# A small product for the sums of the exponentials, its inverse and its broadcast, one slot later

## The chip, the cores and the metric

The kernel runs on one core of a Trainium2 chip. The engines named below are TensorE (PE; its weight loads are a row of their own, PEld), VectorE (DVE), ScalarE (ACT), GpSimd (POOL) and the queue from which most transfers are issued (SP). The metric is the time of one execution on the device in microseconds (us): the median of three runs of the kernel before is 901.06 us.

## The reference

Soft-capped attention, and then a mixing block on its output:

```python
scores = scale * np.matmul(q, k.transpose(0, 1, 3, 2))      # q, k, v: batch 8, heads 12, 448 x 64
scores = cap * np.tanh(scores / cap)
attn = np.exp(scores - max);  attn = attn / (np.sum(attn, axis=-1, keepdims=True) + 1e-09)
x = np.matmul(attn, v)                                      # heads side by side: batch 8, 448 x 768
theta = x @ w_theta
yr = w_tok_r @ (x * cos(theta));  yi = w_tok_i @ (x * sin(theta))
u = x + yr + yi
out = u + np.maximum(u @ w_ch, 0.0)
```

## The kernel before, in words

Two heads make a pair, so there are 48 pairs, six for each of the eight batches. The program is a hand-written pipeline of slots. Slot s computes the scores, the tanh and the exponentials of pair s, and the product with V, the row sums and the normalisation of earlier pairs. Beside that, each slot from the ninth on carries one sixth of the mixing block of one batch that is already through attention. Six slots in a row ("parts" 0 to 5) so hold the mixing block of batch b and the attention of six later pairs.

The order inside a slot is a string of words in `part_scripts`, and the words are emitted in that order; each engine then runs its own instructions strictly in the order in which they were emitted. The words that matter here, with the lines of the profile:

- `SA`, `SB`: the score matmuls of the first and second half of the keys (L262, L279) and their tanh on ACT (L297); `SB` emits the matmuls and `tB` the tanh. `A`, `B`: the exponentials on ACT (L308, L303, L305).
- `V`: the product of the exponentials with V for the pair before (L368); `x` copies it out (L387); `v` loads a further V from ACT's queue (L232).
- `a`, `b` and `a-`, `b-`: the exponentials are added up over the blocks of keys on DVE (L332, L334) and reduced to `part` (L322). The words with a minus do it for the pair of the slot before. `c`, `c-`: for every second pair, the rest of the keys is reduced (L322, `rest`) and added into `part` (L356).
- `r`: a small product on PE (L400, 56 x 32 out) that finishes the row sums of two pairs from `part`. `inv`: their reciprocal on DVE (L436) and a transfer of 7 KB to a buffer in HBM (L441). `bc`: four transfers that read that buffer back, broadcast to 128 partitions (L457). `norm`: two multiplications on DVE that use them (L461).
- `prep`: DVE splits the next queries and keys into a high and a low part (L221, L222). `q`, `q+`: loads of queries and keys on SP (L209).
- `mix0` to `mix5`: the six mixing products of the batch, 21 matmuls each (L545 to L547), from `zh` (`high`, ACT, L531) and `zl` (`low`, DVE, L537); `gain0` to `gain5` add them to x on DVE (L551), `us` splits the sum for the last product (L471, L472), `ch` is that last product.

PE's outputs `r`, `mx`, `th`, `ch` and the product with V of odd pairs share one pool of three PSUM buffers, in the order of emission; a product waits until the buffer of the third one before it has been read.

Of the kernel before, what the change touches and what calls it, by code (L numbers as in the profile page):

```python
# [36 lines left out]
def softcap_attn_then_spectral_mix(ctx, tc, qk2, v, vj, cap, w_theta, w_tok, w_ch, sel, outT):  # L37
    nc = tc.nc
    B, NP, P, _, S = qk2.shape
# [155 lines left out]
    vt, pt, bc = {}, {}, {}  # L195
# [186 lines left out]
    def copy_x(k):  # L382
        if joint(k) and k % 2 == 0:
            return
        for n in (k - 1, k) if joint(k) else (k,):
            x = wk.tile([P, S], F32, tag="x", name=f"x{n}", bufs=12)
            nc.scalar.copy(x, ACC.pop(n)[:, :S])  # L387
            X[n // NP, n % NP] = x
# [3 lines left out]
    def direct(k):  # L392
        return k < DIRECT and not state["general"]

    def sums(k, halves=(0, 1)):

        if not direct(k):
            if k % 2 == 1 and 0 in halves:
                state["r"] = psM.tile([P, 512], F32, tag="m", name=f"r{k}")
                nc.tensor.matmul(state["r"][: 4 * TB, :32], parts.pop(k).rearrange("p n t -> p (n t)"), sel_sb, start=True, stop=True)  # L400
            return
        alone = NP <= k
        if not alone and k % 2 == 0:
            return
        if (k % 2 == 0 or not alone) and 0 in halves:
            state["r"] = psM.tile([P, 512], F32, tag="m", name=f"r{k}")
        r = state["r"]
        for c in range(NCH):
            if c // 2 in halves:
                for n in (k,) if alone else (k - 1, k):  # L410
                    for hh in range(2):
                        i = 2 * (n % 2) + hh
                        nc.tensor.matmul(r[32 * i : 32 * i + 32, :S], ones_sb, pt[n, c // 2][:CP, c % 2, hh, :],
                                         start=c == 0, stop=c == NCH - 1)
# [5 lines left out]
    def invert(k):  # L420

        if k % 2 == 0:
            return
        r = state.pop("r")
        ri = wk.tile([4 * TB, 32], F32, tag="rq", name=f"rq{k}", bufs=1)
        if direct(k):
            rows = wk.tile([P, S + D], F32, tag="ri", name=f"ri{k}", bufs=1)[:, :S]
            nc.vector.tensor_copy(rows, r[:, :S])
            nc.sync.dma_start(ri, rows[::32, :].rearrange("n (t i) -> n t i", i=32))
            summed[k] = ri  # L430
            return
        if state["general"]:
            nc.vector.tensor_scalar_add(ri, r[: 4 * TB, :32], 1e-9)
            nc.vector.reciprocal(ri, ri)
        else:
            nc.vector.reciprocal(ri, r[: 4 * TB, :32])  # L436
        keep(k, ri)

    def keep(k, ri):
        inverse[k] = dram.tile([2, 2, S], F32, tag="inverse", name=f"inverse{k}")  # L440
        nc.sync.dma_start(inverse[k].rearrange("n h (t i) -> (n h t) i", i=32), ri)  # L441

    def inverted(k):
        if k in summed:
            ri = summed.pop(k)
            nc.vector.reciprocal(ri, ri)
            keep(k, ri)

    def spread(k):
        inverted(k)  # L450
        if k not in inverse:
            return
        rows = inverse.pop(k)
        for n in (k - 1, k):
            bc[n] = wk.tile([P, S], F32, tag="bc", name=f"bc{n}", bufs=2)
            for hh in range(2):
                nc.sync.dma_start(bc[n][hh * D : (hh + 1) * D, :], rows[n % 2, hh : hh + 1, :].broadcast_to([D, S]))  # L457

    def norm(k):
        x = X[k // NP, k % NP]  # L460
        nc.vector.tensor_tensor(x, bc.pop(k), x, op=ALU.mult)  # L461
# [104 lines left out]
    def part_scripts(b):  # L566
        rows = [
# [9 lines left out]
        ]  # L577
        if b == 0:
            rows = [
# [9 lines left out]
            ]  # L589
        return [row.split() for row in rows]  # L590
# [75 lines left out]
    def slot(s):  # L666
        k = s - 1
        b, part = divmod(s - FIRST, 6) if s <= NS else (B - 1, None)
        live = s < NS
        tail = k < NS  # L670
        tanh = {}

        def do(e):
            if e == "SA" and live:
                qk_half(s, 0)()
            if e == "SAm" and live:
                tanh["A"] = qk_half(s, 0)
            if e == "tA" and live:
                tanh["A"]()
            if e == "V" and tail:  # L680
                av(k)
            if e == "x" and tail:
                copy_x(k)
            if e == "v" and s + 1 < NS:
                load_v(s + 1)
            if e == "r" and tail:
                sums(k)
            if e == "inv" and tail:
                invert(k)
            if e == "bc" and tail:  # L690
                spread(k)
            if e == "SB" and live:
                tanh[0] = qk_half(s, 1)
            if e == "tB" and live:
                tanh[0]()
            if e == "prep" and WHOLE <= s + 1 < NS:
                split_qk(s + 1)
            if e == "q":
                if s >= WHOLE:
                    if live and s % 2 == 0:  # L700
                        load_ends(s)
                    if s % 2 == 1 and s + 1 < NS:
                        load_qk(s + 1)
                elif s + 2 < NS:
                    load_qk(s + 2)
            if e == "q+" and s >= WHOLE and s + 2 < NS:
                load_qk(s + 2)
            if e in ("wa", "wb", "wc", "wd", "we"):
                weights(s, e[1])
            if e in ("A", "B") and live:  # L710
                exp_half(s, "AB".index(e))
            if e in ("a", "b") and live:
                add_half(s, "ab".index(e))
            if e in ("a-", "b-") and tail:
                add_half(k, "ab".index(e[0]))
            if e == "c" and live:
                add_ends(s)
            if e == "c-" and tail:
                add_ends(k)
            if e == "norm":  # L720
                if s % 2 == 1 and s < NS:
                    norm(s - 3)
                    norm(s - 2)
                if s == NS:
                    norm(s - 2)
                    norm(s - 1)
                    for j in range(NJ):
                        split_x(B - 1, j, "xs")

        for e in TAIL[s - NS - 1].split() if s > NS else part_scripts(b)[part]:  # L730
            name = e.rstrip("0123456789")
            if name in WORK:
                WORK[name](b, int(e[len(name):]))
            else:
                do(e)
# [76 lines left out]
```

## Time and profile before

| | |
|---|---|
| median of 3 runs | 901.06 us (899.86 to 902.13) |
| the profiled execution | 905.79 us, of which the trace spans 904.0 us |
| TensorE's mean granted clock in it | 0.989 of full speed |
| busy: PE, PEld, DVE, ACT | 878.6, 644.6, 658.3, 562.9 us |

Busy times are unions of the instructions of an engine. A matmul's end is modelled, so that matmuls that follow each other closely overlap in the trace: their pace is read from their starts. An idle time stands in square brackets behind an instruction in a timeline, with what ended it.

### The profile page before, as it was taken

How to read it: one execution, taken by the hardware profiler on the slowest of the kernel's cores; microseconds unless marked ns; L12 is line 12 of the kernel's file. 1: busy time of each engine (PE TensorE's matmuls, PEld its weight loads, DVE VectorE, ACT ScalarE, POOL GpSimd, SP SyncE). 2: the span in 40 equal slices, each digit the busy share in tenths (PEclk: the TensorE clock that was granted, in tenths of full speed). 3: DMA queues.
4: the chain of work that ended last, by engine and by line, in shares of the span. 5: the costliest groups of instructions: out<-in, count | busy, mean ns of one | idle time of the engine just before them, and what ended most of it. 6: DMA issues, size and time to landing. Idle time of an engine off the chain costs nothing.

```text
span 904.0 us, 12434 instructions
## 1 busy us (share of the span) xinstructions
PE 878.6 (97%) x4780; PEld 644.6 (71%) x4780; DVE 658.3 (73%) x940; ACT 562.9 (62%) x582; POOL 1.1 (0%) x7
## 2 busy tenths in 40 slices
PE   8999999999999999999989999999989999999997
PEld 5333766776677776777767777767766776689997
DVE  5888899888775777755986569756787478864851
ACT  6987876668664695556953677446765559554320
POOL 0000000000000000000000000000000000000000
PEclk9999999999999999999999999999999999999999
DMA  7564284325523255222552325423362335501521
GB/s 265 189 202 123 85 279 152 127 95 163 161 77 111 77 183 183 66 100 84 181 168 85 104 100 178 131 84 116 112 191 86 105 95 166 159 15 51 194 82 64
DMA packets 70307, 117.32 MB, mean 130 GB/s; under 512 B 10464, under 2 KB 49888, under 8 KB 70240
## 3 DMA queue, kind: packets, MB, share of 16 engines
q1 hardware_dynamic: 64624, 107.47, 37.2%
q10 hardware_dynamic: 5616, 8.98, 3.4%
q8 instruction: 39, 0.64, 0.3%
q14 instruction: 28, 0.23, 0.1%
HBM read 83.18 MB, written 33.20 MB: 129 GB/s over the span
## 4 chain that ended last, share of the span: by engine, by line
PE 68%; DVE 15%; ACT 6%; DMA 4%; issue 3%; SPq 3%; DVEq 0%; ACTq 0%; POOL 0%; POOLq 0%
PE a L368 8%; PE s L262 7%; PE ch L480 6%; PE ch L482 6%; PE ch L481 6%; PE mx L545 5%; PE mx L546 4%; PE mx L547 4%; PE th L480 4%; PE th L481 4%; PE th L482 4%; DVE g_sb L508 4%; DMA g_sb<-turn 3%; DVE g_sb L515 3%; ACT p L297 3%
## 5 line engine op out<-in xcount | busy, mean ns | idle before, releaser
L297 ACT ACTIVATE p<-s,qscale 128x1792 f32<-128x1792 f32 (+1 forms) x96 | 153.6, 1600 | 145.4 <-PE s L262 117.2
L545 PE MATMUL mx<-wtk_h,zh 128*128 128x448 f32 x336 | 124.4, 370 | 0.0
L547 PE MATMUL mx<-wtk_h,zl 128*128 128x448 f32 x336 | 122.8, 366 | 0.0
L546 PE MATMUL mx<-wtk_l,zh 128*128 128x448 f32 x336 | 122.8, 365 | 0.0
L480 PE MATMUL th<-xs,wth_h 128*128 128x448 f32 x288 | 106.7, 370 | 0.0
L480 PE MATMUL ch<-us,wch_h 128*128 128x448 f32 x288 | 106.6, 370 | 0.0
L482 PE MATMUL ch<-us,wch_l 128*128 128x448 f32 x288 | 105.3, 366 | 0.2 <-DVE wch_l L138 0.2
L481 PE MATMUL ch<-us,wch_h 128*128 128x448 f32 x288 | 105.2, 365 | 0.0
L482 PE MATMUL th<-xs,wth_l 128*128 128x448 f32 x288 | 105.2, 365 | 0.0
L481 PE MATMUL th<-xs,wth_h 128*128 128x448 f32 x288 | 105.2, 365 | 0.0
L368 PE MATMUL a<-p,v 128*64 128x448 f32 x480 | 104.5, 573 | 0.0
L308 ACT ACTIVATE p<-p,cap_sb 128x1792 f32<-128x1792 f32 (+1 forms) x56 | 100.0, 1785 | 0.5
L559 DVE SCALAR_TENSOR_TENSOR x<-ch,x 128x448 f32<-128x448 f32 x48 | 29.7, 619 | 75.1 <-PE ch L482 75.1
L537 DVE TENSOR_TENSOR zl<-g_sb,zh 128x896 fp32r<-128x896 f32 x48 | 51.6, 1084 | 33.9 <-ACT zh L531 30.5
L368 PEld LDWEIGHTS a<-p,v 128*64 128x64 f32 x480 | 32.5, 144 | 56.0 <-issue 44.6
L545 PEld LDWEIGHTS mx<-wtk_h,zh 128*128 128x128 f32 x336 | 63.1, 188 | 12.4 <-issue 3.6
L508 DVE TENSOR_TENSOR g_sb<-g_sb,x 128x896 f32<-128x896 f32 x48 | 51.7, 1077 | 27.2 <-ACT g_sb L504 27.2
L547 PEld LDWEIGHTS mx<-wtk_h,zl 128*128 128x128 f32 x336 | 63.1, 188 | 5.2
L546 PEld LDWEIGHTS mx<-wtk_l,zh 128*128 128x128 f32 x336 | 63.1, 188 | 4.9
L480 PEld LDWEIGHTS th<-xs,wth_h 128*128 128x128 f32 x288 | 54.1, 188 | 11.7 <-issue 4.9
L480 PEld LDWEIGHTS ch<-us,wch_h 128*128 128x128 f32 x288 | 54.1, 188 | 10.6 <-issue 5.1
L531 ACT CAST zh<-g_sb 128x896 fp32r<-128x896 f32 x48 | 44.8, 939 | 25.8 <-PE mx L546 13.2
(103 smaller groups left out, 1450.3 us busy)
## 6 DMA issues: line engine op xcount, KB each, us to landing
turn<-g_sb SPq DMA_DIRECT2D x48, 448.0 KB
g_sb<-turn SPq DMA_DIRECT2D x192, 112.0 KB
qk_sb<-in_qk SPq DMA_DIRECT2D x39, 448.0 KB
bc<-inverse SPq DMA_DIRECT2D x96, 112.0 KB
out_dram<-x SPq DMA_DIRECT2D x48, 224.0 KB
v<-in_vj ACTq DMA_DIRECT2D x20, 256.0 KB
g_sb<-in_wth SPq DMA_DIRECT2D x6, 768.0 KB
ends<-in_qk SPq DMA_DIRECT2D x17, 256.0 KB
```

The lines of the kernel that those rows point to most:

```text
L262: nc.tensor.matmul(sp[:, i, hh, :S], kk[k][rows, 1, at : at + P], qq[k][rows, 0, :], start=n == 0, stop=n == 2)
L297: return lambda: nc.scalar.activation(pp[rows, :n], sp[rows, :n, :, :S], AF.Tanh, scale=qscale[rows])
L308: nc.scalar.activation(pp[rows], pp[rows], AF.Exp, scale=cap_sb[rows])
L368: nc.tensor.matmul(acc[hh * D : (hh + 1) * D, :S], va[:, c, hh, :], pt[k, c // 2][:, c % 2, hh, :], start=c == 0, stop=False)
L480: nc.tensor.matmul(acc[:, :S], wh[:, j, ms], t[:, 0, :], start=j == 0, stop=False)
L481: nc.tensor.matmul(acc[:, :S], wh[:, j, ms], t[:, 1, :], start=False, stop=False)
L482: nc.tensor.matmul(acc[:, :S], wl[:, j, ms], t[:, 0, :], start=False, stop=j == NJ - 1)
L508: nc.vector.tensor_tensor(g, g, X[b, j].unsqueeze(1).broadcast_to([P, 2, S]), op=ALU.mult)
L537: nc.vector.tensor_tensor(zl.rearrange("p c (g t) -> p c g t", g=4), turned(j), zh.bitcast(F32).rearrange("p c (g t) -> p c g t", g=4), op ...
L545: nc.tensor.matmul(acc[:, :S], zh[:, c, :], wtk_h[:, c, :], start=c == 0, stop=False)
L546: nc.tensor.matmul(acc[:, :S], zh[:, c, :], wtk_l[:, c, :], start=False, stop=False)
L547: nc.tensor.matmul(acc[:, :S], zl[:, c, :], wtk_h[:, c, :], start=False, stop=c == NC2 - 1)
```

## The change

It touches the scripts of parts 2 and 3 for batches 1 to 6 (batch 0 and the tail have scripts of their own). The words `r inv bc` leave the end of part 2 and stand in part 3 as `r- a inv- bc-`: the product behind `mix3`, the fourth mixing product; the reciprocal behind `a`; the broadcast behind that. `prep` moves from ahead of `gain3` to behind `us0`. Nothing is computed that was not computed before, and no instruction is added or taken away.

```diff
             "SA high0 low0 high1 sincos1 low1 b- V x v SB mix0 high2 rotate3 turn3 low2 gain0 tB q rotate4 turn4 back3 prep"
-            " rotate5 turn5 back4 back5 A B mix1 gain1 c- mix2 r inv bc",
-            "SA a- gain2 high3 low3 V x v high4 low4 SB tB q b- A mix3 a high5 low5 prep gain3 us0 q+"
+            " rotate5 turn5 back4 back5 A B mix1 gain1 c- mix2",
+            "SA a- gain2 high3 low3 V x v high4 low4 SB tB q b- A mix3 r- a inv- bc- high5 low5 gain3 us0 prep q+"
             " B mix4 b c gain4 us1 us2 norm mix5",
...
+            if e == "r-":
+                sums(k - 1)
+            if e == "inv-":
+                invert(k - 1)
+            if e == "bc-":
+                spread(k - 1)
```

On PE, at the first of the six places, the kernel before has the small product (`r`) between the last matmuls of `mix2` (`mx_2`) and the scores of the next slot (`s`):

```order
L545 MATMUL mx_2_1907<-wtk_h,zh_2_1842 128x448
L546 MATMUL mx_2_1907<-wtk_l,zh_2_1842 128x448
L547 MATMUL mx_2_1907<-wtk_h,zl_2_1848 128x448
L400 MATMUL r_1929<-sel_sb,part_1598 56x32
L262 MATMUL s<-hi_1862 128x448 x2
```

In the changed kernel the scores follow `mix2` at once, and at the end of `mix3` (`mx_3`), ahead of `mix4` (`mx_4`), the same engine has:

```order
L545 MATMUL mx_3_1979<-wtk_h,zh_3_1945 128x448
L546 MATMUL mx_3_1979<-wtk_l,zh_3_1945 128x448
L547 MATMUL mx_3_1979<-wtk_h,zl_3_1947 128x448
L400 MATMUL r_2001<-sel_sb,part_1598 56x32
L545 MATMUL mx_4_2029<-wtk_h,zh_4_1958 128x448
```

The product has moved behind the scores, the product with V and `mix3`.

On DVE the kernel before has, from the reciprocal (`rq`) on to `gain3` (the second `x`; the first is `gain2`):

```order
L436 RECIPROCAL rq_1931<-r_1929 56x32
L332 TENSOR_TENSOR psz<-p_0_1782 128x896
L551 TENSOR_TENSOR x_936<-mx_2_1907,x_936 128x448
L537 TENSOR_TENSOR zl_3_1959<-g_sb_94,zh_3_1957 128x896
L537 TENSOR_TENSOR zl_4_1972<-g_sb_94,zh_4_1970 128x896
L334 TENSOR_TENSOR psz<-psz,p_1_1819 128x896
L322 TENSOR_REDUCE part_1987<-psz 128x28
L332 TENSOR_TENSOR psz<-p_0_1953 128x896
L537 TENSOR_TENSOR zl_5_2016<-g_sb_94,zh_5_2014 128x896
L221 CAST hi_2018<-qk_sb 128x896
L222 TENSOR_TENSOR lo_2019<-qk_sb,hi_2018 128x896
L551 TENSOR_TENSOR x_938<-mx_3_1991,x_938 128x448
```

The changed kernel has there:

```order
L332 TENSOR_TENSOR psz<-p_0_1782 128x896
L551 TENSOR_TENSOR x_936<-mx_2_1907,x_936 128x448
L537 TENSOR_TENSOR zl_3_1947<-g_sb_94,zh_3_1945 128x896
L537 TENSOR_TENSOR zl_4_1960<-g_sb_94,zh_4_1958 128x896
L334 TENSOR_TENSOR psz<-psz,p_1_1819 128x896
L322 TENSOR_REDUCE part_1975<-psz 128x28
L332 TENSOR_TENSOR psz<-p_0_1941 128x896
L436 RECIPROCAL rq_2004<-r_2001 56x32
L537 TENSOR_TENSOR zl_5_2016<-g_sb_94,zh_5_2014 128x896
L551 TENSOR_TENSOR x_938<-mx_3_1979,x_938 128x448
L472 TENSOR_TENSOR us_0_2019<-x_567,us_0_2019 128x448
L221 CAST hi_2022<-qk_sb 128x896
```

The reciprocal has moved down by seven instructions, and `hi` and `lo` (the word `prep`) now stand behind `gain3` and the first `us`.

On SP's queue, as a difference from the kernel before, behind the last transfers of the rotated values (`turn`):

```order
 L523 DMA g_sb_94<-turn_5_1868 32x4x224 x4
-L441 DMA inverse_1933<-rq_1931 56x32
-L457 DMA bc_1935<-inverse_1933 64x448 x2
-L457 DMA bc_1938<-inverse_1933 64x448 x2
-L209 DMA qk_sb<-in_qk 128x896 x2
+L209 DMA qk_sb<-in_qk 128x896
+L441 DMA inverse_2006<-rq_2004 56x32
+L457 DMA bc_2008<-inverse_2006 64x448 x2
+L457 DMA bc_2011<-inverse_2006 64x448 x2
+L209 DMA qk_sb<-in_qk 128x896
```

The inverse and its four broadcasts have moved from ahead of the slot's two loads of queries and keys to between them.

## Rows read from the trace of the kernel before

**Rows 1.** The page: busy time, share of the span and instructions of each engine.
```profile
PE 878.6 (97%) x4780; PEld 644.6 (71%) x4780; DVE 658.3 (73%) x940; ACT 562.9 (62%) x582; POOL 1.1 (0%) x7
```

**Rows 2.** Waits of PE: us in total, times, longest.
```profile
PE r L400 <- DVE part L356: 14.7, 6, 3.0
```

**Rows 3.** Timeline of PE, first and fifth place: start, us, instruction [idle before].
```profile
239.05 0.37 PE L547 MATMUL mx<-wtk_h,zl 128*128 128x448 f32 x1
241.45 0.29 PE L400 MATMUL r<-sel_sb,part 128*56 128x32 f32 x2 [2.04 <-DVE part L356]
241.67 0.47 PE L262 MATMUL s<-hi 64*128 64x448 f32 x2
...
672.09 0.37 PE L547 MATMUL mx<-wtk_h,zl 128*128 128x448 f32 x1
675.41 0.29 PE L400 MATMUL r<-sel_sb,part 128*56 128x32 f32 x2 [2.96 <-DVE part L356]
```

**Rows 4.** Windows from the scores to `mix3`: us, busy, PEclk, DMA share, GB/s.
```profile
241.67:248.80 7.13, 7.13 (x41) 3.08 (x39) 3.17 (x5) 3.52 (x3) 0.00 (x0) 0.76 0.57 154
350.20:357.41 7.21, 7.21 (x41) 3.00 (x39) 3.16 (x5) 3.52 (x3) 0.00 (x0) 0.76 0.52 152
458.92:464.46 5.54, 5.54 (x40) 2.52 (x38) 3.07 (x4) 3.02 (x3) 0.00 (x0) 1.00 0.63 170
566.35:573.47 7.12, 7.12 (x41) 3.31 (x39) 3.15 (x5) 3.52 (x3) 0.00 (x0) 0.76 0.57 141
675.63:682.74 7.11, 7.11 (x41) 3.33 (x39) 3.18 (x5) 3.52 (x3) 0.00 (x0) 0.76 0.54 150
783.74:790.91 7.17, 7.17 (x40) 2.98 (x38) 4.98 (x6) 3.42 (x3) 0.00 (x0) 0.76 0.52 150
```

**Rows 5.** Timeline of PE where scores follow a mixing product directly.
```profile
261.71 0.37 PE L547 MATMUL mx<-wtk_h,zl 128*128 128x448 f32 x1
262.01 0.47 PE L262 MATMUL s<-hi 64*128 64x448 f32 x2
```

**Rows 6.** Timeline of DVE, third place.
```profile
458.25 0.40 DVE L356 TENSOR_TENSOR part<-part,rest 64x28 f32<-64x28 f32 x2
459.03 0.35 DVE L436 RECIPROCAL rq<-r 56x32 f32<-56x32 f32 x1 [0.38 <-PE r L400]
...
463.06 1.09 DVE L537 TENSOR_TENSOR zl<-g_sb,zh 128x896 fp32r<-128x896 f32 x1 [2.03 <-ACT zh L531]
...
468.35 1.09 DVE L332 TENSOR_TENSOR psz<-p 128x896 f32<-128x896 f32 x1
...
470.81 0.62 DVE L221 CAST hi<-qk_sb 128x896 fp32r<-128x896 f32 x1
...
472.47 0.62 DVE L551 TENSOR_TENSOR x<-mx,x 128x448 f32<-128x448 f32 x1
...
478.83 1.16 DVE L461 TENSOR_TENSOR x<-bc,x 128x448 f32<-128x448 f32 x2
...
483.73 1.70 DVE L472 TENSOR_TENSOR us<-x,us 128x448 fp32r<-128x448 f32 x3 [3.21 <-ACT us L471]
```

**Rows 7.** Timeline of PE, third place: end of `mix4`, start of `mix5`.
```profile
472.88 0.36 PE L547 MATMUL mx<-wtk_h,zl 128*128 128x448 f32 x1
473.08 0.36 PE L545 MATMUL mx<-wtk_h,zh 128*128 128x448 f32 x1
```

**Rows 8.** Timeline of SP's queue, first place.
```profile
244.17 0.36 SPq L441 DMA_DIRECT2D inverse<-rq  x1
246.36 3.35 SPq L457 DMA_DIRECT2D bc<-inverse  x4
249.81 7.54 SPq L209 DMA_DIRECT2D qk_sb<-in_qk  x2
```

**Rows 9.** Timeline of DVE: reciprocal and `norm` of the next two pairs.
```profile
269.95 0.35 DVE L436 RECIPROCAL rq<-r 56x32 f32<-56x32 f32 x1
...
279.56 1.15 DVE L461 TENSOR_TENSOR x<-bc,x 128x448 f32<-128x448 f32 x2
```

## The prediction

> **What bounds the kernel now.** I read four views, from coarse to fine. The busy times come first: PE is busy for 97% of the span, DVE for 73% and ACT for 62% [rows 1]. The reader is to see that a change pays only if PE waits less, or runs faster while it is busy. So the second view is the list of PE's waits. One entry stands out: the small product `r` waits six times for `part`, the last of DVE's row sums, 14.7 us in all and 3.0 us at most [rows 2]. The third is PE's timeline around one such wait. The last matmul of `mix2` starts at 239.05, then PE is idle for 2.04 us until DVE has written `part`, `r` runs at 241.45, and the next scores start at 241.67 [rows 3]. Nothing in those scores needs `r`; they stand behind it only because PE runs in order. The fourth view is the windows from those scores to `mix3`. The same matmuls take 5.54 us at the third place, where the granted clock is 1.00, and 7.11 to 7.21 us at the other five, where it is 0.76, a mean of full speed and of half of it [rows 4]. Of TensorE's two levels, 1.2 and 2.4 GHz, the lower one was granted for a part of these stretches, right behind the idle time. So each wait costs twice: once as idle time, and at five of six places again as slow matmuls.
>
> **The change part by part.** A place is one of the six batches, 1 to 6, in which the moved words stand.
>
> *The wait of `r` goes.* Without it the scores start 0.30 us after the last matmul of a mixing product, as they do where they follow one directly [rows 5]. Before, they start 241.67 - 239.05 = 2.62 us after it, that is 2.32 us later: the idle 2.04 and 0.28 for the modelled end of the last matmul and for `r` itself. For six places that is 14.7 + 6 x 0.28 = 16.4 us.
>
> *`r` is paid elsewhere.* It runs between `mix3` and `mix4`. From its start to that of the next matmul is 0.22 us [rows 3], a change of form costs 0.30 instead of 0.20 us from start to start [rows 5, 7], and 0.20 would have passed anyhow: 0.22 + 0.30 - 0.20 = 0.3 us, 1.9 us for six. If its two changes of form cost double it is 0.5 and 3 us. `part` was then written some 8 us ago, and the PSUM buffer it takes is that of `mix1`, read long before. It waits for neither.
>
> *The clock's second cost goes.* Five stretches against the one at full clock: 1.59 + 1.67 + 1.58 + 1.57 + 1.63 = 8.0 us [rows 4]. If the idle time goes, I expect these stretches to take 5.54 us.
> The Trainium skill (TensorE: Matmul & The Clock Gate, "Why this matters for your kernels") warns that PE's idle gaps between bursts of matmuls drop its clock, but it names a longer gap than any of the six here. By that rule none of them would have cost the clock, the fall would have another cause that stays, and this term would be nothing. The trace shows the fall behind five of the six gaps, 2.0 to 3.0 us long, and I go by the trace; the other case is a rival below.
>
> *What is late next on DVE.* DVE is behind PE at this point, and the change does not make it faster. The scores start up to 3 us earlier against DVE's work, so I count from their start, S. The third place, which has no slow clock, is the model (S = 458.92). There `zl3` ends at 464.15, S + 5.2; DVE had waited 2.03 us for ACT's `zh3`, which so came at S + 4.1 [rows 6]. In the changed kernel DVE ends its sums later against S: at the fifth place S would be 672.09 + 0.30, the sums end at 675.41, S + 3.0 [rows 3]. Then come `a-` (1.09) and `gain2` (0.62), both lengths from [rows 6], so `zl3` starts at S + 4.7 instead of S + 4.1 and ends at S + 5.8. `mix3` starts at S + 5.54, and `zl3` is first read by its third matmul, near S + 6.0. The cover is the 2.03 us of idle time; 0.2 us of it are left at the worst place, so small waits are possible but not a new gap of 2 us.
>
> *The reciprocal and `prep`.* `inv` leaves the head of that queue (0.35 us and 0.38 of waiting [rows 6]) and stands behind `a`, at S + 9.4 in the model. `r` is done near S + 10.2 (5.54, then 21 matmuls at 0.2, then 0.3), `a` at S + 10.5: no wait of note. Behind it wait `zl5` and `gain3`. `mix5` now takes the PSUM buffer of `mix3`, not that of `r`, so `gain3` must end before `mix5` starts, which is a wait that the change adds. In the model `gain3` ends at 473.09 and `mix5` starts at 473.08 [rows 6, 7]: kept so, it would be a close thing. But `prep` (1.7 us, from 470.81 to the model's `gain3` at 472.47) is moved behind `gain3`. From `a` at S + 9.4 I count 1.09, 0.73 for `inv`, 1.09 for `zl5` and 0.62: `gain3` ends near S + 13.2 with some tenths for ACT's `zh5`, and `mix5` starts at 473.08 - 458.92 + 0.3 = S + 14.5. `prep` ends 0.6 + 1.7 us later, S + 15.5; the next slot's scores need it at S + 14.5 + 4.5 = S + 19.
>
> *SP's queue.* The inverse and its four broadcasts (2.2 us from the issue of the one to that of the others, then 3.35 us of issuing [rows 8]) go between the two loads of queries and keys. The first load gets ahead of them, the second gets behind; its data are wanted a slot later. Who waits for the broadcasts is `norm`. Before, it came 478.83 - 459.38 = 19.4 us after the reciprocal; now `inv` ends about 1.8 us after `a` starts, and `norm` follows `a` by 10.5 us plus the 0.7 inserted: 9.4 us are left. The same chain is followed by a `norm` 9.26 us after the reciprocal, without a wait, at another part [rows 9], so that much was enough there. If it is late, `gain5` and then the splits `us` wait behind it, but DVE idles 3.21 us right there for ACT [rows 6].
>
> *The sum.* Saved: 16.4 - 1.9 + 8.0 = 22.5 us; I take back 0.7 us for small waits at `mix3` and `mix5` (bounds: 0, and 1 us at each place, 6 us). Against the profiled execution, 905.79 us, that is 884.0; that execution lies 4.7 us above the median of the runs, 901.06, from which the same sum gives 879.3 us.
>
> **The rivals.**
>
> *The clock falls all the same.* Then 16.4 - 1.9 - 0.7 = 13.8 us are saved and the time is 887 us. For it: a gap of 2.54 us at the third place did not bring the fall, so a gap alone does not decide. Against it: all five slow windows stand directly behind such a gap.
>
> *The wait moves to `mix3` or `mix5`.* DVE is behind by up to 3 us and recovers in a stretch with 2 us of idle time. If `zl3`, or `zh4` and `zh5` behind their transfers, come 1.5 us later than I counted, six new gaps cost 9 us, and with a slow clock behind half of them another 3 x 1.6: 888 to 893 us. Against it: the third place shows 2.03 us of slack.
>
> *Slower than before: the broadcasts come too late for `norm`.* It is one mechanism: inverse to HBM, then four broadcasts, all behind a load on SP's queue and now begun nine to ten microseconds later against `norm`. From 9.4 us on DVE waits; from 9.4 + 3.2 = 12.6 us on the splits, and so the last product on PE, wait; a loss begins where that takes 22.5 / 6 = 3.75 us at every place, so from a chain of 16.4 us. At 18 us the time would be 901 + 6 x 1.6 = 911 us. Against it: 9.26 us were enough [rows 9].
>
> *It does not do what it says:* `r` waits again at its new place, for a buffer or for `part`, and the time stays at 901 us. Against it: `mix1` and `part` are finished a whole product earlier.
>
> **How the numbers follow.** My forecast, 877 to 883 us, gets 0.74; the wait that moves 0.10; the clock that falls all the same 0.08; no effect 0.04; slower 0.04. The likeliest case gives 879.3 us. The range goes from 876 (no small waits, and a clock a little better) to 889, which takes in the clock case and the cheap half of the moved wait. What a measurement of this kernel can tell from no change is about 0.3%, 2.7 us. All cases but the last two are faster by more than that: 0.92 faster, 0.04 the same, 0.04 slower.
>
> **What would show it.** In the profile of the changed kernel the entry of PE waiting at `r` for `part` should be gone from the waits, and no other wait of PE should reach 1 us at these places. The windows from the scores to `mix3` should all take about 5.5 us with a clock of 1.00, and the mean clock of the span should rise from 0.989. DVE's idle time ahead of `zl3` should shrink from 2 us to a few tenths, and its idle time at the splits `us` should stay. The prediction is wrong in its clock term if windows with 0.76 remain without a gap ahead of them; in its first term if PE waits at `mix3`, `mix5` or the last product for as long as it waited at `r`.

## The result, and the profile after

The changed kernel takes 884.64 us, the median of four runs (883.96 to 885.37), against 900.46 us for the kernel before in the same comparison: a ratio of 0.9824, 95% interval [0.9804, 0.9844], so 14 to 18 us less. Run once more later beside other kernels (`e10` below) it took 884.52 us against 901.84: 0.9801 [0.9776, 0.9825]. Forecast were 879.3 us and a range of 876 to 889. The sign and the range held; the likeliest value promised some 5 us too much.

The profiled execution took 884.27 us, 21.5 us less than that of before. Its page begins, as in [rows 1], with the busy times and their shares of the span:

```profile
span 882.5 us, 12440 instructions
PE 872.5 (99%) x4780; PEld 641.5 (73%) x4780; DVE 657.0 (74%) x940; ACT 562.6 (64%) x582; POOL 1.1 (0%) x7
```

PE is busy for 99% of a shorter span; the busy time of the others is what it was. The list of PE's waits, of which [rows 2] was the first line, now is, as a whole:

```profile
PE s L252 <- ACT p L297: 3.2, 7, 1.9
PE fill L93 <- POOL ones_sb L98: 0.9, 1, 0.9
PE s L271 <- ACT p L297: 0.5, 2, 0.2
PE ch L482 <- DVE wch_l L138: 0.2, 1, 0.2
```

The wait of `r` is gone, and none has come in its place: what is left belongs to the first 90 us and one weight. PE's timeline at the fifth place, which had the longest gap of the six [rows 3] (start, length, instruction):

```profile
656.67 0.37 PE L547 MATMUL mx<-wtk_h,zl 128*128 128x448 f32 x1
656.97 0.47 PE L262 MATMUL s<-hi 64*128 64x448 f32 x2
...
666.75 0.37 PE L547 MATMUL mx<-wtk_h,zl 128*128 128x448 f32 x1
667.05 0.29 PE L400 MATMUL r<-sel_sb,part 128*56 128x32 f32 x2
667.27 0.47 PE L545 MATMUL mx<-wtk_h,zh 128*128 128x448 f32 x1
667.58 0.37 PE L546 MATMUL mx<-wtk_l,zh 128*128 128x448 f32 x1
...
671.63 0.36 PE L545 MATMUL mx<-wtk_h,zh 128*128 128x448 f32 x1
```

The scores follow `mix2` after 0.30 us. From the last matmul of `mix3` to the second of `mix4` it is 0.30 + 0.22 + 0.31 = 0.83 us, where two steps of 0.20 would have stood without `r`: it costs 0.4 us there. `mix5` starts at S + 14.66, with S = 656.97. The windows from the scores to `mix3`, of which [rows 4] had five at a clock of 0.76, three of the six (length, busy times, then clock, DMA share, GB/s):

```profile
238.09:243.64 5.55, 5.55 (x40) 2.54 (x39) 4.71 (x8) 2.79 (x3) 0.00 (x0) 1.00 0.78 222
447.53:453.08 5.55, 5.55 (x40) 2.54 (x39) 5.27 (x8) 2.58 (x2) 0.00 (x0) 1.00 0.73 226
761.69:767.24 5.55, 5.55 (x40) 2.54 (x39) 4.71 (x8) 2.77 (x3) 0.00 (x0) 1.00 0.79 235
```

All six take 5.55 us at a granted clock of 1.00. DVE's timeline at the fifth place shows where its idle time went; the rows answer to [rows 6]:

```profile
658.63 0.40 DVE L356 TENSOR_TENSOR part<-part,rest 64x28 f32<-64x28 f32 x2
...
661.12 1.09 DVE L537 TENSOR_TENSOR zl<-g_sb,zh 128x896 fp32r<-128x896 f32 x1 [0.44 <-ACT zh L531]
...
668.01 0.34 DVE L436 RECIPROCAL rq<-r 56x32 f32<-56x32 f32 x1
668.28 1.02 DVE L537 TENSOR_TENSOR zl<-g_sb,zh 128x896 fp32r<-128x896 f32 x1
669.23 0.60 DVE L551 TENSOR_TENSOR x<-mx,x 128x448 f32<-128x448 f32 x1
...
670.29 0.61 DVE L221 CAST hi<-qk_sb 128x896 fp32r<-128x896 f32 x1
...
677.24 1.15 DVE L461 TENSOR_TENSOR x<-bc,x 128x448 f32<-128x448 f32 x2
...
682.28 1.16 DVE L472 TENSOR_TENSOR us<-x,us 128x448 fp32r<-128x448 f32 x2 [3.36 <-ACT us L471]
```

`part` is complete at S + 2.1, `zl3` ends at S + 5.2 with 0.44 us of idle time ahead of it instead of 2, `gain3` ends at S + 12.9, 1.8 us before `mix5`, `norm` comes 8.9 us after the reciprocal without a wait, and 3.36 us of idle time are left at the splits. SP's queue at the first place, against [rows 8] (start, length, issue):

```profile
243.80 0.35 SPq L209 DMA_DIRECT2D qk_sb<-in_qk  x1
249.13 0.33 SPq L441 DMA_DIRECT2D inverse<-rq  x1
250.44 2.38 SPq L457 DMA_DIRECT2D bc<-inverse  x4
252.93 0.52 SPq L209 DMA_DIRECT2D qk_sb<-in_qk  x1
```

The first load of queries and keys is issued at 243.80, ahead of the inverse; before, it was held until 249.81 behind the broadcasts.

So in the traces the six places give nearly what was forecast, 22.5 us: comparing the start of every matmul in the two traces, by its number, 21.9 us are gained between the first and the sixth place. Ahead of them the trace of the changed kernel is 1.3 us shorter, a part that the change does not touch, and behind them 1.7 us longer. But the medians of the runs differ by 16 to 17 us, not by 21.5. The experiments ask where the other 5 us went. Theory A: the profiled execution of before had more of the slow clock than a usual run. Theory B: every run of before has as much, and the change gives some 5 us back somewhere.

### The profile page after: what moved, and what is told of

Same layout as the page of the kernel before. It is cut to its first block, busy times and chain, and to the rows that moved or that the text cites. A ratio compares the mean times of both kernels' runs of the same rounds, so it can differ in the third digit from the quotient of the medians.

```text
span 882.5 us, 12440 instructions
## 1 busy us (share of the span) xinstructions
PE 872.5 (99%) x4780; PEld 641.5 (73%) x4780; DVE 657.0 (74%) x940; ACT 562.6 (64%) x582; POOL 1.1 (0%) x7
## 4 chain that ended last, share of the span: by engine, by line
PE 90%; DVE 4%; ACT 3%; DMA 1%; issue 1%; SPq 1%; ACTq 0%; POOL 0%; DVEq 0%; POOLq 0%
PE a L368 10%; PE s L262 9%; PE mx L545 8%; PE mx L547 7%; PE mx L546 7%; PE ch L480 7%; PE th L480 7%; PE ch L482 6%; PE ch L481 6%; PE th L482 6%; PE th L481 6%; PE s L252 2%; ACT p L297 2%; PE a L374 2%; PE s L279 2%; PE a L379 2%
## 5 line engine op out<-in xcount | busy, mean ns | idle before, releaser
L368 PE MATMUL a<-p,v 128*64 128x448 f32 x480 | 99.0, 548 | 0.0
L545 PEld LDWEIGHTS mx<-wtk_h,zh 128*128 128x128 f32 x336 | 63.2, 188 | 12.6 <-issue 6.8
L491 ACT ACTIVATE g_sb<-th 128x448 f32<-128x448 f32 x48 | 25.9, 539 | 55.4 <-PE th L482 55.4
```

The costliest lines, as they stand in the source:

```text
L368: nc.tensor.matmul(acc[hh * D : (hh + 1) * D, :S], va[:, c, hh, :], pt[k, c // 2][:, c % 2, hh, :], start=c == 0, stop=False)
L545: nc.tensor.matmul(acc[:, :S], zh[:, c, :], wtk_h[:, c, :], start=c == 0, stop=False)
```

## The experiments

Times are medians; kernels of one comparison share the runs of the kernel before, 901.61 us (17 runs) in the first, 901.82 (9) in the second, 901.84 (9) in the third. S is the start of the scores in part 3.

**`e1_prep_only`: one part alone.**

```diff
- ... mix3 a high5 low5 prep gain3 us0 q+ ...
+ ... mix3 a high5 low5 gain3 us0 prep q+ ...
```

> Only prep moves behind us0; r, inv and bc stay at the end of part 2. Both theories (A: the profiled execution of before had more falls of the clock than a usual run; B: every run of before has five, and the change gives some 6 us back elsewhere): r waits for part as before, 14 to 15 us in all, because prep stands behind that place. Time within 0.3% of before, 898 to 903 us. If prep alone carried the gain, it would be 885 us.

Measured: 902.27 us, ratio 1.0008 [0.9989, 1.0027]. PE's longest entry of waits:

```profile
PE r L400 <- DVE part L356: 14.5, 6, 3.2
```

As expected: the wait stays, and so does the time. `prep` carries none of the gain by itself.

**`e2_r_only`: the other part alone** (the changed kernel with `prep` back ahead of `gain3`).

```diff
- ... mix3 r- a inv- bc- high5 low5 gain3 us0 prep q+ ...
+ ... mix3 r- a inv- bc- high5 low5 prep gain3 us0 q+ ...
```

> r, inv and bc move as in the change, prep stays ahead of gain3. mix5 takes the PSUM buffer of mix3, so it needs gain3. In the changed kernel gain3 ends at S + 12.6 to 13.2 and mix5 starts at S + 14.66; with 1.7 us of prep ahead of it gain3 would end at S + 14.3 to 14.9. Expected: waits of PE at mix5 of 0 to 0.3 us a place, 0 to 2 us in all, time 884.5 to 886.5 us. Rival: mix5 waits over 1 us a place and the clock falls behind it, 892 us or more.

Measured: 884.72 us, 0.9812 [0.9793, 0.9831], the time of the change. DVE at its fifth place, where `mix4` starts at 668.10 and, 4.35 us on, `mix5`:

```profile
669.76 0.62 DVE L221 CAST hi<-qk_sb 128x896 fp32r<-128x896 f32 x1
...
671.42 0.62 DVE L551 TENSOR_TENSOR x<-mx,x 128x448 f32<-128x448 f32 x1
```

`gain3` ends at 672.04, 0.4 us before `mix5` needs it; at the third place, where it is closest, 0.1 us are left. Moving `prep` was a precaution that this kernel does not need, by a small margin; the gain comes with `r`, `inv` and `bc`.

**`e3_fill_gap`: the wait stays, PE does not idle in it.** The kernel before, with needless matmuls ahead of `r` into its own tile:

```diff
+                for _ in range(warm):          # 11 at the six places
+                    nc.tensor.matmul(state["r"][:32, :CP], ones_sb, ones_sb[:, :1].broadcast_to([CP, CP]), start=True, stop=True)
                 nc.tensor.matmul(state["r"][: 4 * TB, :32], parts.pop(k)...
```

> The kernel before with 11 needless small matmuls (32x112, ones by ones, into the tile of r, which r then overwrites) ahead of r at the six places: they fill about 2.1 us of the 2 to 3 us for which PE waits for part, and leave the wait itself. If idle time brings the fall of the clock, it does not fall: mean clock 1.00, the windows from the scores to mix3 at 5.5 us. By theory A the usual run of before has about two falls of 1.6 us, so the time is 896.5 to 898.5 us; by theory B it has five, and the time is 892 to 893 us. If the fall has another cause, clock and time stay as before, 899 to 902 us.

Measured: 896.72 us (894.77 to 897.96), 0.9940 [0.9922, 0.9959], at a mean clock of 0.999 to 1.000 in all six runs. Two of its windows from the scores to `mix3` (all six read alike) and what PE still waits at `r`:

```profile
241.05:246.60 5.55, 5.55 (x41) 2.57 (x39) 3.07 (x4) 3.51 (x3) 0.00 (x0) 1.00 0.65 180
670.00:675.54 5.54, 5.54 (x40) 2.52 (x38) 3.07 (x4) 3.51 (x3) 0.00 (x0) 1.00 0.67 184
```
```profile
PE r L402 <- DVE part L356: 2.0, 2, 1.1
```

This shows two things. The fall of the clock comes with PE's idle time and goes with it, though PE gets to the scores no earlier. And in usual runs it costs 4.9 us (3.7 to 7.0 by the interval), not the 8.0 us that the profiled execution showed; some tenths more if one allows for the needless matmuls, with which the six stretches from `mix2` to the scores are longer by 0.7 us in sum (18.9 against 18.2). The clock that each run lists points the same way: over 35 runs of the kernel before, it is 0.992 in the median (0.990 to 0.996), and the time falls by 1.0 us for each 0.001 by which it is higher; the profiled execution stood at 0.989, below all of them. The trace of `e1`, which waits as before and has the usual clock of 0.992, shows four falls, worth 6.6 us; here are its third and fourth place:

```profile
458.53:465.76 7.23, 7.23 (x40) 2.97 (x38) 3.16 (x5) 3.52 (x3) 0.00 (x0) 0.76 0.53 135
566.79:572.33 5.54, 5.54 (x40) 2.54 (x39) 3.17 (x5) 3.52 (x3) 0.00 (x0) 1.00 0.68 188
```

The third, which kept its clock before, fell behind a gap of 2.95 us, and the fourth, which had fallen, did not behind 2.06 us. So Theory A holds, for 3 us by the middle of `e3` and for 1 to 4 us by its interval.

**`e4_c_early`: another way to end the wait.** The last sums move ahead in DVE's queue; `r`, `inv` and `bc` stay where they were.

```diff
- ... low1 b- V x v SB mix0 ... mix1 gain1 c- mix2 r inv bc
+ ... low1 b- c- V x v SB mix0 ... mix1 gain1 mix2 r inv bc
```

> r, inv and bc stay at the end of part 2, but the last sums (c-: rest and the two additions to part, 1.5 us of DVE) are moved from behind gain1 to directly behind b-, some 10 us earlier in DVE's queue. If r waits only because part stands late in DVE's queue, r no longer waits and the time is that of the change, 883 to 887 us, without moving r. Rival: the 1.5 us are only handed on; rotate3 to rotate5 and their transfers come 1 to 1.5 us later, mix3 or mix4 waits for zh or zl, and 3 to 9 us of the gain are lost, 888 to 894 us.

Measured: 890.77 us, 0.9865 [0.9844, 0.9887]. The time is in the rival's range, but the wait is not where the rival put it. `r` no longer waits for `part`, and PE now waits at the last product, 5.7 us at five places, 1.5 us of it at the first, where the clock falls behind it. SP's queue, DVE and PE at that place:

```profile
245.66 0.36 SPq L441 DMA_DIRECT2D inverse<-rq  x1
248.43 2.37 SPq L457 DMA_DIRECT2D bc<-inverse  x4
250.90 6.31 SPq L209 DMA_DIRECT2D qk_sb<-in_qk  x2
```
```profile
255.07 0.63 DVE L221 CAST hi<-qk_sb 128x896 fp32r<-128x896 f32 x1 [3.29 <-DMA qk_sb<-in_qk]
...
264.17 0.62 DVE L551 TENSOR_TENSOR x<-mx,x 128x448 f32<-128x448 f32 x1
```
```profile
264.84 0.47 PE L480 MATMUL ch<-us,wch_h 128*128 128x448 f32 x1 [1.51 <-DVE x L551]
265.16 0.36 PE L481 MATMUL ch<-us,wch_h 128*128 128x448 f32 x1
...
266.04 0.58 PE L481 MATMUL ch<-us,wch_h 128*128 128x448 f32 x1
```

The last row shows the slower clock: the same matmul takes 0.58 instead of 0.36 us. The load of the next queries and keys stands behind the inverse and its broadcasts and is issued at 250.90. DVE waits 3.29 us for it with `prep`, all behind `prep` is late by that, and `gain5` frees the PSUM buffer for the last product too late. Before, the same queue was nearly as late (249.81, [rows 8]), but PE was late too. That it was the queue and not DVE's load is what `e9` tests.

**`e5_r_after_v`: `r` earlier in the slot.** Part 3 of the changed kernel with `V r- x v inv- bc-` behind `low3`, and without them behind `mix3`.

> r stands directly behind V in part 3 (some 3.8 us after the scores begin, S + 3.8), inv and bc behind low3; the rest as in the changed kernel. part was written by S + 2.7 at the latest there, so r should not wait: no gap over 0.3 us at the six places, mean clock 1.00, 883.5 to 886 us, as in the change. If r must stand behind a whole mixing product to be free, waits of part remain and the time is over 888 us.

Measured: 883.65 us, 0.9791 [0.9769, 0.9813]; no wait of PE at `r`, `mix3` or the last product. As expected: `r` need not stand behind the fourth product, only behind the moment when `part` is written.

**`e6_r_after_scores`: `r` too early.** `SA r- inv- bc- a- gain2 ...` in part 3.

> r, inv and bc stand directly behind the six score matmuls of part 3, at S + 1.4. In the changed kernel part is written at S + 2.0 to S + 2.7. So r should wait 0.6 to 1.3 us at each place, 4 to 7 us in all, and the time is 888 to 892 us; gaps that short should not bring the lower clock often (mean 0.998 or more). If the lag of DVE at these places follows PE (it stands still when PE does), r waits as long as in before, 2 to 3 us, and the time is 897 us or more.

Measured: 886.31 us, 0.9829 [0.9805, 0.9853], with a mean clock of 0.998 to 1.000. The wait is back, shorter, as the lag of DVE less the scores' own 1.4 us would have it:

```profile
PE r L400 <- DVE part L356: 4.4, 6, 1.1
```

The time lies 2 us below what was expected: the wait was at the low end of the 4 to 7 us, no fall of the clock came with gaps of 0.6 to 1.1 us in the trace, and the last products go at the faster of two paces, which the next experiments are about.

**`e7_tail_112` and `e8_tail_56`: the pace of the last products.** In the trace of the changed kernel the 450 or so matmuls from the last `r` (784.02) to the end start 206.7 ns apart, in that of before 202.7, at a clock of 1.00 in both. Three rows of the changed kernel, and three of `e7`, the changed kernel with one needless matmul behind that last `r`:

```diff
+                if s == NS:
+                    nc.tensor.matmul(state["r"][:32, 256 : 256 + 112], ones_sb, ones_sb[:, :1].broadcast_to([CP, 112]), start=True, stop=True)
```
```profile
819.65 0.37 PE L480 MATMUL ch<-us,wch_h 128*128 128x448 f32 x1
...
820.27 0.37 PE L480 MATMUL ch<-us,wch_h 128*128 128x448 f32 x1
...
820.89 0.37 PE L480 MATMUL ch<-us,wch_h 128*128 128x448 f32 x1
```
```profile
819.81 0.36 PE L480 MATMUL ch<-us,wch_h 128*128 128x448 f32 x1
820.02 0.36 PE L481 MATMUL ch<-us,wch_h 128*128 128x448 f32 x1
...
820.83 0.36 PE L482 MATMUL ch<-us,wch_l 128*128 128x448 f32 x1
```

In the first, 1.24 us lie between the outer rows, six matmuls; in the second 1.02 us, five, which is 0.207 against 0.204 a matmul (202.7 ns over the stretch).

> The changed kernel with one needless matmul of 112 columns behind the last r, ahead of the last 480 or so matmuls (into columns of r's tile that nothing reads). In the changed kernel those run at 206.7 ns from start to start, in before at 202.7. If the pace is set where a run of products begins, by how its start falls, it may jump to 202.7: 1.9 us less, 882.5 to 883.5 us. If the pace belongs to the kernel's data or transfers in that stretch, it stays at 206.7 and the time is 884.5 to 885.5 us.

> The same with 56 columns. If the pace of the tail is set by how the start of the run falls, this one and the one with 112 columns may differ; if a matmul in between is what matters, both have the same pace; if neither matters, both are at 206.7 ns and 884.5 to 885.5 us.

Measured: 883.45 us, 0.9796 [0.9774, 0.9817], and 884.24 us, 0.9797 [0.9775, 0.9818]. Both traces show 202.7 ns in the tail. So a matmul in between is enough, 112 or 56 columns alike, and the slower pace belongs to how that run of matmuls begins, not to its data or transfers. The same tail keeps 202.7 ns without an added matmul in the traces of `e1`, `e3` to `e6` and `e9`, and 206.7 in those of the changed kernel and `e2`, the two that have `r` between `mix3` and `mix4`. By the traces the slower pace costs 450 x 4 ns = 1.8 us. The times show 0.3 to 1.1 us against `e10`, which is inside their spread. What in the beginning sets the pace stays open.

**`e9_c_early_bc`: `e4` with the broadcasts behind the load.**

```diff
- ... mix1 gain1 mix2 r inv bc                        SA a- ... SB tB q b- A mix3 ...
+ ... mix1 gain1 mix2 r inv                           SA a- ... SB tB q bc- b- A mix3 ...
```

> As the one with c- directly behind b- and r, inv at the end of part 2, but with the four broadcasts behind the first load of queries and keys on SP's queue (bc- behind q in part 3), as the change has it. There prep waited 3.29 us for that load, issued at 250.90 behind the broadcasts, gain3 to gain5 stood behind prep, and the last product waited up to 1.6 us. If the queue was the cause, prep does not wait, no wait of PE at the last product is over 0.3 us, and the time is 882 to 885 us. If DVE's own load is the cause (1.5 us of sums ahead of rotate3), the waits at the last product stay and the time is 888 to 891 us.

Measured: 882.32 us (881.32 to 882.60), 0.9776 [0.9752, 0.9801]. SP's queue and DVE at the first place:

```profile
246.11 0.36 SPq L441 DMA_DIRECT2D inverse<-rq  x1
246.57 0.36 SPq L209 DMA_DIRECT2D qk_sb<-in_qk  x1
249.39 2.37 SPq L457 DMA_DIRECT2D bc<-inverse  x4
```
```profile
252.38 0.62 DVE L221 CAST hi<-qk_sb 128x896 fp32r<-128x896 f32 x1
```

The load is issued 4.3 us earlier, `prep` does not wait, PE waits nowhere behind the opening, and 8.4 us against `e4`, which ran in another comparison, are back. The queue was the cause of the waits; about 1 us of the 8.4 is pace, for in the trace of `e4` five runs of the last product go at 206.7 ns. `e9` is also the fastest version tried, 2.2 us below the changed kernel in the same comparison: its slowest run (882.60) lies below the other's fastest (883.42). Two things in its trace are better. The mixing products and the tail behind the six places run at 202.7 ns. And `r`, back between `mix2` and the scores, costs less there:

```profile
656.48 0.37 PE L547 MATMUL mx<-wtk_h,zl 128*128 128x448 f32 x1
656.77 0.29 PE L400 MATMUL r<-sel_sb,part 128*56 128x32 f32 x2
656.99 0.47 PE L262 MATMUL s<-hi 64*128 64x448 f32 x2
```

The scores start 0.51 us after `mix2` instead of 0.30: 0.2 us a place, half of what `r` costs in the midst of the mixing products, where the form changes twice for it alone.

**`e10_after_again`: the changed kernel once more.**

> The changed kernel once more, beside the one with the early sums on the same chip: 884 to 885.5 us, a mean clock of 0.999 to 1.000, no wait of PE over 0.3 us behind the opening; the products of the tail at 206.7 ns from start to start, if that pace belongs to the program (202.7 if it falls differently from run to run).

Measured: 884.52 us, 0.9801 [0.9776, 0.9825], mean clock 0.998 to 1.000. Its trace has 206.7 ns in the tail again, so for the tail the pace goes with the program. That does not hold for every run of matmuls: `mix3` at the first place keeps 206.7 ns in the first trace of this kernel and 202.7 in this one.

## Why the prediction was right or wrong

- *The wait of `r` goes* (16.4 us): right. The scores start 0.30 us after `mix2` at all six places.
- *`r` is paid elsewhere* (0.3 us a place, 1.9 in all): too low. It counted one change of form, and PE pays one into `r` and one out of it: 0.4 us a place, 2.5 in all, inside the 3 us that the text allowed for this.
- *The clock's second cost goes* (8.0 us): the mechanism was right, the size was not. The windows are at 5.55 us and 1.00, and `e3` ties the fall to the idle time. But the term was read from one execution with five falls, and then subtracted from the median of the runs. The text itself said that this execution lay 4.7 us above the median, and used that only as an offset, where it was a sign that its clock was not the usual one. In usual runs the term is 4.9 us (3.7 to 7.0). This is the mis-sized step: about 3 of the 5 us.
- The rival *the clock falls all the same* failed: the clock is 1.00 here, and in `e3` too, where only the idle time was filled.
- *What is late next on DVE*: right. `zl3` was forecast to end by S + 5.8 at the worst place; it ended at S + 5.2 to 5.4, with 0 to 0.46 us of idle time ahead of it. The 0.7 us taken back for small waits were not needed. The rival of a wait that moves to `mix3` or `mix5` failed with it.
- *The reciprocal and `prep`*: `gain3` was forecast at S + 13.2 and ended at S + 12.6 to 13.2. The move of `prep` was priced as the cover for it; `e2` shows that 0.1 to 0.4 us would have been left without.
- *SP's queue*: the forecast said that the first load gets ahead and priced that at nothing. How much it can be worth is shown by `e4` against `e9`, 8.4 us, with `r` at its old place. With `r` moved, the load was not tried behind the broadcasts, so what the order gives to this change is not shown. `norm` did not wait; the rival that ends slower needed a chain of 16.4 us and 9 were shown.
- Not foreseen: the slower pace of the last products, 1.8 us in the trace. It is the second part of the missing 5 us; that much the change does give back elsewhere, as Theory B had it. With 16.4 us for the idle time, -2.5 for `r`, 4.9 for the clock and -1.8 for the pace the sum is 17.0 us; `e10` measured 17.3 us, the first comparison 15.8. So the terms add up as far as can be seen with a clock term that is known to lie between 3.7 and 7.0 us.

## What to carry to other kernels

A small instruction that waits for a slow engine holds up all that stands behind it on an engine that runs in order; it can stand later at a small cost (0.4 us of PE a place here, and 0.2 us in `e9`, where the form of the matmuls changes anyway), as long as nothing before its new place needs it, and how much later is read from the lag of the engine it waits for (here 2 to 3 us). Once such a wait is gone, the next one can be in a queue that was late all along under its cover, as in `e4`, so the order of the transfers has to be looked at with it. A term that rests on a state of the chip which differs from run to run, as the clock does here, has to be sized by the runs that the result is compared with, not by the one execution that was profiled.

## What the runs showed of the hardware

- PE's clock fell to the lower level behind five of six gaps of 2.0 to 3.0 us in the profiled execution of before, behind four of six gaps of 2.0 to 3.2 us in `e1`, and behind one of two gaps of 1.5 to 1.6 us in `e4`. It did not behind six gaps of 0.6 to 1.1 us in `e6`, nor behind a gap of 1.85 us in the opening, which all twelve traces have. So the length of a gap alone does not decide, and a place that has the fall in one execution may not have it in another: the mean clock is 0.990 to 0.996 over 35 runs of one kernel.
- Runs of the same 128 x 128 by 448 matmuls keep one of two paces, 202.7 or 206.7 ns from start to start, at a granted clock of 1.00, from the beginning of a run of matmuls to its end. Of the 547 runs of at least 15 such matmuls in the twelve traces, 77 keep the slower one, and none lies between 203.0 and 206.4 ns. The slower one costs 2%. One more small matmul ahead of the tail changed which (`e7`, `e8`).
